# Dummy products in the idle time of TensorE, and a recalibrated queue model, in the prologue of a fused attention and MLP kernel

## The chip, the cores and the metric

One core of a Trainium2 chip. The metric is device time in microseconds (us) of one execution. The kernel before was quoted at 1057.43 us (median of 3 executions, 1055.95 to 1057.48). Every execution also lists its span and the mean granted clock of TensorE (1.0 is full speed).

## The reference, cut to what matters

```python
x = A_x                                   # (1, 2048, 1024) bf16
xn = layernorm(x)                         # no scale, no shift
qkv = xn @ wqkv                           # 32 heads of 32
p = softmax((q @ k^T) * 32**-0.5)         # over 2048 keys, per head
s = (p @ v) @ wo
g = silu(gelu_tanh(layernorm(xn) @ w1 + b1) @ w2 + b2)     # 3584 hidden
return x + s * g
```

The exponentials of the softmax, 32 x 2048 x 2048 of them, run on ScalarE as 1024 instructions of 128 x 1024. They are what the whole kernel is built around.

## The kernel before

The kernel does not write its instructions in order. Every operation is added to a plan; at build time the plan is list-scheduled (step by step, each engine is given the best operation that is ready) with a model of each engine's time, semaphore waits are placed, and each engine then gets its instructions in the order that the model found. **The model decides only the order.** Each engine is handed its list in that order, and in the traces it waits where data is missing (TensorE 0.82 us at 44.79 for a transposing transfer).

The model of a DMA transfer is one queue of a fixed rate and a landing time by kind:

```python
# in _Plan.run(), commit():
if e == "SP":
    ...
    tf[e] = t + o.occ
    state["bw"] = max(state["bw"], t) + o.nbytes / 380.0
    o.fin = state["bw"] + {"w1": WLAT, "w2": WLAT, "tp": 2400.0, "x0": 1900.0, "x1": 1900.0}.get(o.sem[:2], 2300.0)
```

and TensorE takes, at each step of model time `t`, the best candidate that is ready, or sleeps until the next one will be (`nxt`):

```python
# pe_step(t), cut:
for c in cands:
    if c[0] <= t: ...                       # ready: keep the best class
    else:         nxt = min(nxt, c[0])
...
if best is None:
    if nxt < INF:
        wake(nxt, "PE")
    return
```

The prologue turns x into the first keys, queries and values. Sixteen tiles of 128 rows are loaded; VectorE makes their statistics; the normalised tile goes into a ring of four buffers (the profile calls three of them `gw` and one `yT`); tiles 0 and 1 are transposed by TensorE against an identity, tiles 2 to 15 by a transposing DMA into `big`; TensorE then makes K (and Q) of a pair of tiles and V:

```python
for t in (lo, lo + 1):
    if t in DN:        # tiles 2, 3
        xnop[t] = dve(... xnb[t % 4], xst[t] ..., 360, ...)
        continue
    xnop[t] = pool(... xnb[t % 4], xst[t] ..., 950, ...)
for t in (lo, lo + 1):
    ...
    add("SP", lambda e, t=t: e.dma_start_transpose(out=xnT[:, :, t * 128:(t + 1) * 128], in_=xnb[t % 4]),
        1290, 0, [("xnb", t % 4)], [("xnT", t, h) for h in range(2)], 0, sem=f"tp{t % 4}", nbytes=262144)
pro_q.append(k_pair_item(n, False))
...
```

Each engine's list is then issued as it stands:

```python
def emit(self, e, eng, sems):
    for o in self.order[e]:
        for s, v in self.waits[o]:
            eng.wait_ge(sems[s], v)
        ins = o.fn(eng)
        ...
```

The first thing that TensorE does is a warm-up of 13 identity products (`warm_item`). The same DMA queue, that of SyncE, also carries the weights of the MLP. The first six loads of W1 (three pairs of 256 KB each) are held back until a certain tile is normalised, so that they do not crowd the loads of x:

```python
def load_w1(p):
    ...
    for i in range(2):
        ...
        dma(f"w1{gi}{i}", ..., 332000, [], [("w1", gi, i)], 3,
            [xnop[XW + 2 * p]] if p < 3 else [])      # XW = 9: tiles 9, 11, 13
```

After the prologue the first "full unit" of scores starts; from there exponentials, scores, P·V, projections and the MLP run interleaved.

The softmax here doesn't subtract the row's maximum and nothing guards it: scores larger than these inputs give would overflow.

## Time and profile before

| | kernel before |
|---|---|
| span of the profiled execution | 1055.8 us |
| start of the exponentials without a break (first full unit) | 64.6 us |
| from there to the end | 991.2 us |
| TensorE busy from 24.2 to 64.6 us | 38.42 of 40.40 us |
| transposing transfers, issue to landing: least, median, most | 2.9, 4.3, 5.6 us |

The views by stretch, of ScalarE's waits and of TensorE's timeline are in the prediction below. Here is SyncE's part from 36 us on, in the kernel before (start and length of the issuing, line, kind, output and input, how many):

```profile
36.35 1.93 SPq L933 DMA_DIRECT2D w1r<-in_B_w_dram  x2
38.33 0.51 SPq L940 DMA_DIRECT2D w2r<-in_B_w_dram  x1
38.88 3.98 SPq L894 DMA_TRANSPOSE big<-gw  x2
42.90 0.58 SPq L933 DMA_DIRECT2D w1r<-in_B_w_dram  x1
43.52 1.24 SPq L894 DMA_TRANSPOSE big<-gw  x1
44.81 1.34 SPq L894 DMA_TRANSPOSE big<-yT  x1
```

Two blocks of W1 and one of W2, for an MLP whose first product starts at 65.3 us, are issued ahead of the transposes of tiles 12 and 13, and one more W1 ahead of those of 14 and 15. The two transposes at 38.88 took 3.98 us to issue, where the one at 43.52 took 1.24. Their data had been ready: GpSimd's normalisation of tiles 12 and 13 (2.37 us from 35.78 on, on its timeline) ended at 38.15. TensorE's wait at 44.79 (in the prediction's fence) is for these two, tiles 12 and 13, which are pair 6. (The prediction says tile 14 there; that was a slip in counting, for tile 14's transpose is the row at 43.52.)

### The profile page before, as it was taken

Reading aid. Unit: us, or ns where it says so; the run is one execution under the profiler, and the core shown is the slowest. Engines: PE = TensorE matmul, PEld = TensorE weight load, DVE = VectorE, ACT = ScalarE, POOL = GpSimd, SP = SyncE. Lnnn points to the kernel's source line nnn. Section 1 sums busy time; section 2 is a strip of 40 time slices with the busy share of each in tenths; the row PEclk is TensorE's granted clock in tenths of the full one; section 3 lists DMA queues with packets and bytes.
Section 4 is the critical chain, followed back from the end, with each engine's and each line's share of the span. In section 5 each row is a group of like instructions: output and inputs, shape, how many; then the busy total and the mean of one; then the engine's idle time right before and its main releaser. Section 6 shows DMA issues by size and latency. Waiting matters only on the chain.

```text
span 1055.8 us, 31978 instructions
## 1 busy us (share of the span) xinstructions
PE 1024.0 (97%) x14230; PEld 632.8 (60%) x14230; DVE 967.9 (92%) x1463; ACT 1010.3 (96%) x1100; POOL 28.6 (3%) x40
## 2 busy tenths in 40 slices
PE   7998999999999999999999999999999999899997
PEld 4565457656666566656765666556665566564442
DVE  7579899999999989999999999999899999978997
ACT  2779999999999999999999999999999999999994
POOL 3600000000000000000000000000000000000000
PEclk8999999999999999999999999999999999999999
DMA  8955256634275446633565556433664687663322
GB/s 219 232 153 156 56 144 198 184 97 117 86 219 155 135 139 188 166 89 100 160 177 143 146 159 190 135 90 99 179 196 141 192 238 206 193 195 111 124 88 71
DMA packets 302371, 160.16 MB, mean 152 GB/s; under 512 B 40218, under 2 KB 293146, under 8 KB 302234
## 3 DMA queue, kind: packets, MB, share of 16 engines
q1 hardware_dynamic: 302234, 158.12, 53.3%
q8 instruction: 112, 1.84, 0.7%
q14 instruction: 25, 0.20, 0.1%
HBM read 142.35 MB, written 12.06 MB: 146 GB/s over the span
## 4 chain that ended last, share of the span: by engine, by line
ACT 88%; PE 7%; DMA 2%; DVE 2%; SPq 0%; POOL 0%; issue 0%; DVEq 0%; POOLq 0%
ACT P L1134 82%; ACT ut L995 5%; PE ps L701 5%; ACT gw L1031 1%; PE ps L696 1%; PE ps L1120 1%; DMA big<-yT 1%; DMA hT<-in_A_x_dram 1%; DVE ut L854 0%; DMA big<-gw 0%; DVE w1r L1281 0%; DVE V L771 0%; SPq L715 0%; POOL gw L886 0%; SPq L723 0%
## 5 line engine op out<-in xcount | busy, mean ns | idle before, releaser
L1134 ACT ACTIVATE P<-ps 128x1024 bf16<-128x1024 f32 x1024 | 965.3, 1245 | 23.4 <-PE ps L1120 23.3
L1164 DVE TENSOR_TENSOR PA<-P 128x2048 bf16<-128x2048 bf16 x246 | 298.7, 1216 | 15.8 <-ACT P L1134 15.1
L701 PE MATMUL ps<-yT,w1r 128*128 128x256 bf16 x1792 | 231.4, 274 | 3.4 <-DVE nv L1217 1.6
L701 PE MATMUL ps<-w2r,hT 128*128 128x256 bf16 x1792 | 227.2, 274 | 1.6 <-DVE hT L998 0.9
L701 PEld LDWEIGHTS ps<-yT,w1r 128*128 128x128 bf16 x1792 | 162.5, 98 | 58.9 <-issue 30.2
L701 PEld LDWEIGHTS ps<-w2r,hT 128*128 128x128 bf16 x1792 | 162.2, 98 | 53.0 <-issue 31.2
L696 PE MATMUL ps<-P,V 128*32 128x256 bf16 x4096 | 146.5, 274 | 0.0
L1169 DVE TENSOR_TENSOR PA<-PA 128x1024 bf16<-128x1024 bf16 x204 | 138.2, 681 | 1.5
L701 PE MATMUL ps<-big,qk 128*128 128x512 bf16 (+2 forms) x568 | 134.6, 368 | 1.5 <-DMA big<-gw 0.8
L701 PE MATMUL ps<-qk,big 128*128 128x256 bf16 (+1 forms) x736 | 127.3, 306 | 3.2 <-DMA big<-gw 2.7
L696 PEld LDWEIGHTS ps<-P,V 128*32 128x32 bf16 x4096 | 96.5, 96 | 35.6 <-issue 22.6
L1120 PE MATMUL ps<-qk 32*128 32x256 bf16 x2048 | 106.0, 273 | 8.6 <-ACT P L1134 7.6
L1120 PE MATMUL ps<-QKT 32*128 32x256 bf16 x2048 | 101.7, 273 | 2.7 <-ACT P L1134 2.3
L701 PEld LDWEIGHTS ps<-qk,big 128*128 128x128 bf16 x736 | 64.9, 98 | 45.0 <-issue 17.7
L701 PEld LDWEIGHTS ps<-big,qk 128*128 128x128 bf16 x568 | 50.5, 102 | 52.6 <-issue 16.0
L980 DVE TENSOR_TENSOR xb<-ps,b1T 128x512 bf16<-128x512 f32 x112 | 76.4, 685 | 4.7 <-PE ps L701 4.0
L1120 PEld LDWEIGHTS ps<-qk 32*128 32x128 bf16 x2048 | 31.6, 92 | 75.9 <-ACT P L1134 71.6
L1120 PEld LDWEIGHTS ps<-QKT 32*128 32x128 bf16 x2048 | 30.3, 92 | 71.5 <-ACT P L1134 68.5
L995 ACT ACTIVATE ut<-ut 128x1024 f32<-128x1024 f32 x56 | 72.5, 1295 | 0.0
L998 DVE SCALAR_TENSOR_TENSOR hT<-ut,xb 128x1024 bf16<-128x1024 f32 x56 | 67.9, 1212 | 1.3 <-ACT ut L995 1.0
L993 DVE SCALAR_TENSOR_TENSOR ut<-hT,xb 128x1024 f32<-128x1024 bf16 x56 | 68.0, 1214 | 0.0
L696 PE MATMUL ps<-PA,ones 128*32 128x256 bf16 x896 | 46.4, 275 | 0.0
(79 smaller groups left out, 529.7 us busy)
## 6 DMA issues: line engine op xcount, KB each, us to landing
w1r<-in_B_w_dram SPq DMA_DIRECT2D x224, 256.0 KB, 3.5
w2r<-in_B_w_dram SPq DMA_DIRECT2D x128, 448.0 KB, 4.3
qk<-in_A_wqkv_dram SPq DMA_DIRECT2D x16, 256.0 KB, 3.3
g_scratch<-gw SPq DMA_DIRECT2D x32, 128.0 KB, 3.6
o_scratch<-ot SPq DMA_DIRECT2D x56, 64.0 KB, 3.1
big<-o_scratch SPq DMA_DIRECT2D x28, 128.0 KB, 3.7
hT<-in_A_x_dram SPq DMA_DIRECT2D x10, 256.0 KB, 4.2
qk<-in_A_wqkv_dram SPq DMA_DIRECT2D x4, 512.0 KB, 3.7
```

The source lines that it names most:

```text
L696: ins = e.matmul(dst(j), lhsT=lhsT(j), rhs=rhs(j), start=start, stop=stop, tile_position=(0, 32 * j), skip_group_check=True)
L701: return e.matmul(dst, lhsT=lhsT, rhs=rhs, start=start, stop=stop, skip_group_check=True)
L980: dve(lambda e: e.tensor_tensor(xb_t[i2][:, p % 2].rearrange("p (k t) -> p k t", k=2), bank(it.bank).rearrange("p (k t) -> p k t", k=2), b ...
L993: dve(lambda e, r=r: e.scalar_tensor_tensor(ut_t[i2][:, r], h[:, r], 1.0 / GA, xb[:, r], op0=ALU.add, op1=ALU.mult), c_f32(r.stop - r.star ...
L995: act(lambda e: e.activation(ut_t[i2][:], ut_t[i2][:], ACT.Tanh, scale=GC * GA), c_acts(1024), [("ut", i2, 0), ("ut", i2, 1)], [("ut", i2, ...
L998: dve(lambda e, r=r: e.scalar_tensor_tensor(h[:, r], ut_t[i2][:, r], 1.0, xb[:, r], op0=ALU.add, op1=ALU.mult), c_f32(r.stop - r.start), [ ...
L1031: act(lambda e: e.activation(zh, z, ACT.Tanh, scale=0.5), c_acts(1024), [("z", 0), ("z", 1)], [("zh",)], 1)
L1120: ins = e.matmul(bank(b0[j], kk * 256, (kk + 1) * 256), lhsT=QKT[sl][32 * j:32 * j + 32, 1, kb * 128:(kb + 1) * 128], rhs=QKT[sl][32 * j:3 ...
L1134: x = act(lambda e, h=h: e.activation(P[pi][:, 2 * h:2 * h + 2].rearrange("p j k q -> p (j k q)"), ps[:, pr[h] * 1024:(pr[h] + 1) * 1024], ...
L1164: add2.append(dve(lambda e, p0=p0, a0=a0: e.tensor_tensor(PA_all[:, a0:a0 + 2].rearrange("p u j q -> p (u j) q"), P_all[:, p0:p0 + 2, :, 0 ...
L1169: add4.append(dve(lambda e, a0=a0: e.tensor_tensor(PA[a0], PA[a0], PA[a0 + 1], op=ALU.add), c_b16(1024), [("PA", a0 + 1)], [("PA", a0)], P ...
```

## The change

Intent: in the prologue of the kernel before, TensorE runs two stretches at about half clock (0.53 in the prediction's clock column; called cold below), each behind a stretch in which it was mostly idle (busy 1.06 and 1.05 of 3.40 us). So the scheduler puts dummy products (identity times identity, into a free PSUM bank, never read) where its model sees TensorE idle for over 0.3 us, between 6 and 32 us. At the same time the constants of the DMA model are set to longer times. The core of the diff:

```diff
+FILL = 300
+ADJ2 = 0
@@ commit()
-  o.fin = state["bw"] + {"w1": WLAT, "w2": WLAT, "tp": 2400.0, "x0": 1900.0, "x1": 1900.0}.get(o.sem[:2], 2300.0)
+  o.fin = state["bw"] + {"w1": WLAT, "w2": WLAT, "tp": 2800.0, "x0": 2050.0, "x1": 2000.0, "x2": 2500.0}.get(o.sem[:2], 2300.0)
@@ pe_step()
-  cands.append((o.ready, 1, o, None))
+  late = state["mode"] == "f" and state["dopen"] is not None
+  cands.append((max(o.ready, state["cend"]) + ADJ2 if late else o.ready, 1, o, None))
...
   if best is None:
+      if self.fill and t < 32000 and nxt > t + FILL and (t > 6000 or not self.fill[0].left):
+          bf = bank_for(t)
+          if bf is not None and bf[0] <= t:
+              it = self.fill.pop()
+              best = (t, 3, it.chunks[0], (it, bf[1]))
+  if best is None:
       if nxt < INF:
           wake(nxt, "PE")
@@ load_qk(), load_v(): bytes that the model counts
-  dma(f"wqk{i}", ..., 262144 * 8 // 5, ...)
+  dma(f"wqk{i}", ..., 262144 * 2, ...)
-  dma("wv", ..., 665000, ...)
+  dma("wv", ..., 850000, ...)
@@ prologue
+  plan.fill = [fill_item() for _ in range(80)]     # each one 128x512 identity product
@@ normalisation on VectorE, tiles 0, 1 and tiles 2, 3: ns that the model counts
-  75 + 0.26 * 1024
+  455
-  360
+  455
... (bookkeeping of the fills, and marking unused ones as dead: cut)
```

More of the change, by code (lines that the diff above doesn't have):

```diff
@@ L78, in __init__ @@
         self.skip = []
+        self.fill = []
         self.ring_last = {}
@@ L129, in run @@
         state = {"mode": "c", "bw": 0.0, "s": 0, "pv": 0, "pvopen": [], "dopen": None, "susp": None,
-                 "done": 0.0, "last_bank": 7}
+                 "done": 0.0, "cend": 0.0, "last_bank": 7}
         bank_free = {b: [] for b in (4, 5, 6, 7)}
@@ L386, in pe_step @@
                     state["pv"] += 1
+                elif cls == 3:
+                    o.item.k = 1
                 else:
@@ L389, in pe_step @@
                     heads[opening[2]] += 1
-            if cls == 0:
+            if cls == 3:
+                pass
+            elif cls == 0:
                 state["s"] += 1
@@ L401, in pe_step @@
                 it.k += 1
+                if cls == 1:
+                    state["cend"] = start
                 if it.k == len(it.chunks):
@@ L437, in run @@
                 wake(max(t, soon[e][0][0]), e)
+        for it in self.fill:
+            it.chunks[0].dead = True
+            it.chunks[0].start = it.chunks[0].fin = 0.0
         left = [o for o in self.ops if o.start is None]
@@ L722, in load_qk @@
             src = A_wqkv[:, which * D + hg * 128: which * D + (hg + 1) * 128].rearrange("(c p) n -> p c n", p=128)
-            dma(f"wqk{i}", lambda e: e.dma_start(wqk[i], src), 262144 * 8 // 5, [], [("wqk", i)], 3,
+            dma(f"wqk{i}", lambda e: e.dma_start(wqk[i], src), 262144 * 2, [], [("wqk", i)], 3,
                 [xnop[NT - 1]] if nqk["n"] == 3 else [])
@@ L728, in load_v @@
             src = A_wqkv[:, 2 * D + pr * 256: 2 * D + (pr + 1) * 256].rearrange("(c p) n -> p c n", p=128)
-            dma("wv", lambda e: e.dma_start(wv, src), 665000, [], [("wv",)])
+            dma("wv", lambda e: e.dma_start(wv, src), 850000, [], [("wv",)])
         for t in range(XF):
@@ L809, in warm_item, with fill_item @@
             return it
+        def fill_item():
+            it = _Item("fill")
+            chunk(it, lambda e, b: full(e, bank(b), ident[:], ident[:].unsqueeze(1).to_broadcast([128, 4, 128]), True, True), Q512, [("ident",)])
+            return it
         def qk_tile_item(t):
@@ L867, in bass_recurrent_scan__mha_block__mixer_channel_mlp__prompt_kernel @@
                     dve(lambda e, t=t: e.tensor_scalar(xnb[t], xst[t], mv[:, t, 0:1], lnp[:, t, 1:2],
-                                                       op0=ALU.subtract, op1=ALU.mult), 75 + 0.26 * 1024,
+                                                       op0=ALU.subtract, op1=ALU.mult), 455,
                         [XS(t), ("mv", t), ("rs", 0, t)], [("xnb", t)], 0.5)
@@ L882, in bass_recurrent_scan__mha_block__mixer_channel_mlp__prompt_kernel @@
                     xnop[t] = dve(lambda e, t=t: e.tensor_scalar(xnb[t % 4], xst[t], mv[:, t, 0:1], lnp[:, t, 1:2],
-                                                                 op0=ALU.subtract, op1=ALU.mult), 360,
+                                                                 op0=ALU.subtract, op1=ALU.mult), 455,
                                   [XS(t), ("mv", t), ("rs", n)], [("xnb", t % 4)], 0.5)
```

## The prediction

> **What bounds the kernel now.** I read the page first (busy shares and slices), then the busy time of each engine by stretch, then who waited for whom, then the timeline of TensorE in the first 45 us.
>
> Busy time by stretch; the columns are the stretch, its length, the busy time and number of instructions of PE, PEld, DVE, ACT and POOL, the granted TensorE clock, the DMA share and GB/s:
>
> ```profile
> 0.00:24.20 24.20, 17.52 (x119) 10.86 (x120) 17.75 (x52) 5.04 (x6) 7.72 (x17) 0.86 0.84 216
> 24.20:64.60 40.40, 38.42 (x540) 23.11 (x540) 20.02 (x52) 28.29 (x30) 18.62 (x22) 1.00 0.98 210
> 64.60:1041.70 977.10, 961.09 (x13521) 595.66 (x13524) 920.23 (x1345) 977.01 (x1064) 0.00 (x0) 1.00 0.52 149
> 1041.70:1056.00 14.30, 6.98 (x56) 3.20 (x48) 9.87 (x18) 0.00 (x0) 2.28 (x2) 0.83 0.21 74
> ```
>
> The third line carries the argument: from 64.6 to 1041.7 us ScalarE is busy 977.01 of 977.10 us. Its work there is fixed: 992 exponentials left of the 1024, at 15.58 us for 17 (0.916 us each, in the chain of waits), plus the tanh of the MLP and the gate. So the span is a start of 64.6, a body of 977.1 and a tail of 14.1 us. Only start and tail can move, as long as the body stays saturated.
>
> Waits of ScalarE over the whole run (total us, times, longest):
>
> ```profile
> ACT P L1134 <- PE ps L1120: 23.3, 8, 7.0
> ACT big L845 <- PE ps L834: 7.2, 2, 6.4
> ACT L746 <- PEq L1426: 0.7, 1, 0.7
> ```
>
> All of ScalarE's waits are here, and all lie before 64.6: the exponentials wait for score products, that is for TensorE's prologue.
>
> The timeline of TensorE there (start, length, line, output and operands, how many, idle before and releaser):
>
> ```profile
> 1.38 5.64 PE L701 MATMUL ps<-ident 128*128 128x512 bf16 x13 [1.38 <-DVE ident L741]
> 8.00 0.62 PE L834 MATMUL ps<-ident,gw 128*128 128x128 bf16 x8 [0.98 <-DVE gw L867]
> 9.97 0.86 PE L834 MATMUL ps<-ident,gw 128*128 128x128 bf16 x8 [1.35 <-DVE gw L867]
> 10.62 3.38 PE L701 MATMUL ps<-big,qk 128*128 128x128 bf16 x32
> ...
> 19.04 1.05 PE L701 MATMUL ps<-qk,big 128*128 128x256 bf16 x8 [2.73 <-DMA big<-gw]
> 20.33 3.52 PE L701 MATMUL ps<-big,qk 128*128 128x256 bf16 x16 [0.23 <-DMA big<-yT]
> 23.78 0.42 PE L1120 MATMUL ps<-qk 32*128 32x256 bf16 x8
> 24.13 1.05 PE L701 MATMUL ps<-qk,big 128*128 128x256 bf16 x8
> ...
> 31.52 0.39 PE L701 MATMUL ps<-big,qk 128*128 128x256 bf16 x2 [0.40 <-DMA big<-yT]
> ...
> 44.79 0.39 PE L701 MATMUL ps<-big,qk 128*128 128x256 bf16 x2 [0.82 <-DMA big<-gw]
> ```
>
> Compare the two rows of 128x256: sixteen took 3.52 us at 20.33, eight took 1.05 at 24.13. By (length minus one matmul's latency) over (count minus one), that is (3.52-0.42)/15 = 207 ns against (1.05-0.27)/7 = 111 ns each: the first ran at half speed. Cut at steps of about 3.4 us, the clock column (PE alone: stretch, length, busy, clock, DMA) shows the pattern:
>
> ```profile
> 6.60:10.00 3.40, 1.06 (x11) 1.00 1.00 321
> 10.00:13.40 3.40, 3.40 (x35) 0.53 0.99 332
> 13.40:16.85 3.45, 2.91 (x33) 0.97 0.25 89
> 16.85:20.25 3.40, 1.05 (x8) 1.00 1.01 198
> 20.25:23.70 3.45, 3.37 (x16) 0.53 1.07 169
> ```
>
> A stretch with one microsecond of products is followed by one at about half clock; one with three is followed by full clock. The two cold stretches hold exactly the products on which the first long run of exponentials waits.
>
> [...] Here a transposing transfer lands 2.9 us after issue at best and 4.3 us at the median, and the kernel's model adds 2.4 us to its queue time: low, as the diff assumes.
>
> **The change part by part.**
> Removed: nothing that computes. The program is ordered at build time by a model of all engines, so the edits to the model change the order of instructions and not their work.
>
> 1. Fills. Up to 80 identity products of 512 columns may be put where the model sees TensorE idle for over 0.3 us, a bank free, between 6 and 32 us of model time (the chip starts about 0.7 us later). The gaps over 0.3 us in that range are 0.98 + 1.35 + 2.73 + 0.40 = 5.46 us; at 0.216 us each some 23 fills, and I expect 15 to 30. They lie in idle time and by themselves cost nothing, except an overrun of at most one fill where the model's gap is too long: three or four gaps, half a fill on average, 0.3 to 0.5 us.
> 2. What the fills buy, first cold stretch. The 32 products of 128 columns run at (3.38-0.31)/31 = 99 ns each; the warm pace for 128 columns is about half of 111, 56 ns: 31 x 43 ns = 1.35 us, and (0.86-0.31)/7 = 78 against 56 for 7 of the second eight transposes 0.15. Sum 1.5 us. It gets to the next stage through VectorE: the casts out of PSUM at 12.58 and 14.12 stand in its queue ahead of the normalisation of tiles 2 and 3 (15.13 to 16.12), whose transposing transfers TensorE awaits at 19.04. VectorE idled 0.47 and 0.97 us before these casts, so 1.4 of the 1.5 can pass.
> 3. Second cold stretch. Sixteen at 207 become sixteen at 111: 15 x 96 = 1.4 us, plus 0.15 of the latency (0.42 to 0.27): 1.6 us, directly on the path to the score products at 23.78 and to the long run of exponentials at 24.23.
> 4. Recalibration: tile transfers +100 to +200 ns, transposing ones +400, weight loads 1.10 to 1.38 us and 1.75 to 2.24 us of queue (bytes over 380 per ns), normalisation 341 or 360 to 455 ns (the trace shows 0.53 to 0.54 with its latency). It should stop TensorE from being parked in front of transfers that the model thought landed: 0.40 + 0.82 us at 31.52 and 44.79. I count 0.4 of these 1.2.
> 5. The rule with ADJ2 does nothing: it is a maximum with the start of an earlier product, always in the past, plus zero.
>
> From 24.2 to 64.6 TensorE is busy 38.42 of 40.40 us, so an earlier arrival there should carry through to the first full unit at 64.6. VectorE had 0.86 + 0.47 + 0.80 us of waits for TensorE between 21 and 34 us and so can follow most of it. Sum at 64.6: -1.4 -1.6 -0.4 +0.4 = -3.0 us, perhaps -0.2 more in the tail since a tuned change was presumably kept for its best order: 1057.43 - 3.2 = 1054.2 us.
>
> **The rivals.**
> (a) The saved time turns into a wait for transfers. At 44.79 TensorE waits for the transpose of tile 14, behind a chain of statistics on VectorE, normalisation on GpSimd and the transfer. For it: VectorE is 4.95 of 5 us busy from 25 to 30 us. Against it: that chain passes VectorE's casts of TensorE's results, which come earlier too, and 19.28 us of TensorE work follow 44.7. If it wins, about 1 us is left: 1056.4.
> (b) Fills delay real products. In-order TensorE runs every fill; if the model believes in later transfers than there are (3.5 us issue to landing in the new model, 3.2 to 3.4 in the trace for the first two), fills run past the landing. At 5 extra fills, 1.1 us is lost: 1055.3.
> (c) The new order disturbs the body or tail. Every tie in 977 us is decided anew, and TensorE is 98% busy there. A late score product starves ScalarE, and the 14.1 us tail hangs on 24 output products and VectorE. For: tuned constants stay as they were. Against: zero waits of ScalarE in the body, so there is slack. Plus or minus 1 to 2 us: 1052 to 1057.
> (d) Only the clock phase matters: [...]some executions may already have one cold stretch less. The three times spread by 1.5 us. The gain would then vary by that.
>
> **Range and chances.** Ideal carry-through without overrun and with both parked waits gone gives -1.5 -1.6 -1.2 = -4.3, with a lucky tail -6: 1051.4. (a) with (b), or a bad tail, give 1056.8. Predicted 1054.2 us, 8 in 10 between 1051.4 and 1056.8. Two per cent are 21 us, two thirds of all the time ScalarE waits at all; hardly reachable, and nothing in the change can cost as much unless the body breaks. Faster 0.01, same 0.985, slower 0.005.
>
> **What would show it right or wrong.** After: rows of identity products of 512 columns between 7 and 20 us, 216 ns apart; the clock at 1.00 in all stretches from 7 to 25 us; the 16 products of pair 1 in about 1.95 us; the start of the saturated stretch at 61 to 62 us; ScalarE still without waits until the tail, which stays near 14 us. It is wrong if the clock is full and the saturated stretch still begins at 63.5 or later (rival a or b: look for idle time before DMA-released products, or fills adjacent to ready work), if new ScalarE waits appear after it, or if the tail differs by more than 1 us.

The sum: it came to -3.0 us at 64.6, and with 0.2 us for the tail to 1054.2 us. Of what it reckons with, the traces show the following. The 0.216 us of a product of 512 columns: in the kernel before, five at 60.24 take 1.24 us and one 0.38, (1.24-0.38)/4 = 215 ns. The 56 ns of a product of 128 columns was an estimate, half of the measured 111; the changed kernel then took (1.96-0.22)/31 = 56 ns. The clock: in the kernel before it goes to half at 10.2, back at 13.6, to half at 20.4 and back at 23.9 us. That every fill is run: the changed kernel has 36 identity products of 512 columns, 13 of the warm-up and 23 fills.

## The result, and the profile after

In the first comparison the changed kernel took 1059.43 us (median of 4; 1057.37 to 1060.73) and the kernel before 1057.45 (median of 4; 1055.95 to 1057.48). The ratio is 1.002, with a 95% interval of 1.0002 to 1.0039. All ratios and intervals here are from the fast runs of the same rounds; they are not quite the ratio of the medians that are quoted, nor of the means. The class "within 2%" was right; the gain of 3 us was not there, and 1059.4 lies above the range. A repetition in other rounds gave 1.0002 (experiment e1), so the fair statement is: no gain, and nothing lost that is sure.

The busy time by stretch of the changed kernel, with the columns of the prediction's first fence:

```profile
0.00:24.20 24.20, 21.24 (x159) 11.62 (x159) 19.32 (x56) 7.08 (x9) 8.60 (x18) 1.00 0.93 235
24.20:64.60 40.40, 36.71 (x526) 22.02 (x522) 19.21 (x48) 26.63 (x29) 17.74 (x21) 1.00 0.92 199
64.60:1041.70 977.10, 961.56 (x13540) 596.12 (x13544) 920.23 (x1344) 976.55 (x1064) 0.00 (x0) 1.00 0.52 149
1041.70:1056.00 14.30, 6.50 (x44) 2.73 (x32) 9.40 (x18) 0.00 (x0) 2.28 (x2) 0.84 0.21 75
```

In the first stretch the clock went from 0.86 to 1.00, and 159 products ran where 119 had. In the second, TensorE is busy for 36.71 us instead of 38.42: it came in earlier and then **waited more** (it is idle for 3.69 us of the stretch instead of 1.98). Body and tail are as before (976.55 and 977.01 us of ScalarE; the half microsecond is the earlier start).

TensorE's timeline in the changed kernel, same columns as before (line numbers are 20 to 26 higher):

```profile
1.38 6.84 PE L721 MATMUL ps<-ident 128*128 128x512 bf16 x18 [1.38 <-DVE ident L761]
...
9.78 1.96 PE L721 MATMUL ps<-big,qk 128*128 128x128 bf16 x32
...
14.29 2.55 PE L721 MATMUL ps<-ident 128*128 128x512 bf16 x11
17.11 1.05 PE L721 MATMUL ps<-qk,big 128*128 128x256 bf16 x8 [0.27 <-DMA big<-gw]
19.33 1.92 PE L721 MATMUL ps<-big,qk 128*128 128x256 bf16 x16 [1.18 <-DMA big<-yT]
...
33.82 0.83 PE L721 MATMUL ps<-big,qk 128*128 128x256 bf16 x6 [0.94 <-DMA big<-gw]
...
43.59 0.61 PE L721 MATMUL ps<-big,qk 128*128 128x256 bf16 x4 [1.10 <-DMA big<-gw]
```

The eleven fills at 14.29 run (2.55-0.38)/10 = 217 ns apart, with 0.38 for the latency of one: full clock. The 32 products of 128 columns take 1.96 us (3.38 before), the sixteen of pair 1 take 1.92 (3.52 before). So both cold stretches are gone, by the amounts predicted. But look at the brackets: 1.18 us of waiting for a transposing DMA at 19.33, 0.94 at 33.82, 1.10 at 43.59.

Where the exponentials begin, first long run and first full unit, on ScalarE's timeline; the kernel before:

```profile
24.23 7.44 ACT L1134 ACTIVATE P<-ps 128x1024 bf16<-128x1024 f32 x8 [7.05 <-PE ps L1120]
64.61 12.94 ACT L1134 ACTIVATE P<-ps 128x1024 bf16<-128x1024 f32 x14 [6.43 <-PE ps L1120]
```

and the changed kernel:

```profile
22.06 5.61 ACT L1160 ACTIVATE P<-ps 128x1024 bf16<-128x1024 f32 x6 [7.05 <-PE ps L1146]
64.14 12.94 ACT L1160 ACTIVATE P<-ps 128x1024 bf16<-128x1024 f32 x14 [6.76 <-PE ps L1146]
```

This is the whole result in four rows. The first long run came **2.17 us earlier**, and the first full unit, from which ScalarE never rests, only **0.47 us earlier**. The rest of the 2.17 was lost on the way:

| step of TensorE | before | after | gained so far |
|---|---|---|---|
| first long run of exponentials | 24.23 | 22.06 | 2.17 |
| pair 6 (tiles 12, 13) released by its transposes | 44.79 | 43.59 | 1.20 |
| first full unit (ScalarE's row) | 64.61 | 64.14 | 0.47 |

From the release at 44.79 to the score products of the first full unit (64.17) the kernel before needs 19.38 us; the changed kernel from 43.59 to 63.69, 20.10. The recalibrated order has left 0.7 us more of TensorE's work behind that wait.

The changed kernel has 23 fills (5 of them join the warm-up). Apart from the fills, 106 of the 6054 places of TensorE's list hold another operation than before, 39 of VectorE's, 6 of SyncE's and 2 of GpSimd's, all in the prologue; ScalarE's list is the same. The order of body and tail is identical.

### The profile page after: what moved, and what is told of

It is laid out like the page before. It is cut to its first block, busy times and chain, and to the rows that moved or that the text cites. A ratio compares the mean times of both kernels' runs of the same rounds, so it can differ in the third digit from the quotient of the medians.

```text
span 1055.3 us, 32024 instructions
## 1 busy us (share of the span) xinstructions
PE 1026.0 (97%) x14253; PEld 632.5 (60%) x14253; DVE 968.2 (92%) x1463; ACT 1010.3 (96%) x1100; POOL 28.6 (3%) x40
## 4 chain that ended last, share of the span: by engine, by line
ACT 88%; PE 6%; DVE 3%; DMA 1%; POOL 1%; issue 0%; DVEq 0%; SPq 0%
ACT P L1160 82%; ACT ut L1021 5%; PE ps L721 4%; DVE ut L880 1%; ACT gw L1057 1%; PE ps L716 1%; PE ps L1146 1%; DMA big<-yT 1%; DVE w1r L1307 0%; POOL lnp L934 0%; DMA hT<-in_A_x_dram 0%; DVE lnp L898 0%; DVE V L791 0%; POOL gw L912 0%; DVE mv L882 0%
## 5 line engine op out<-in xcount | busy, mean ns | idle before, releaser
L721 PE MATMUL ps<-big,qk 128*128 128x512 bf16 (+2 forms) x568 | 131.7, 360 | 3.3 <-DMA big<-gw 2.0
L721 PEld LDWEIGHTS ps<-big,qk 128*128 128x128 bf16 x568 | 48.1, 98 | 54.4 <-issue 16.0
```

The lines of the kernel that those rows point to most:

```text
L721: return e.matmul(dst, lhsT=lhsT, rhs=rhs, start=start, stop=stop, skip_group_check=True)
```

## The experiments

The first theory after the result: **T1**, transfers bound the prologue from 24 to 64 us, so that a TensorE which comes earlier waits longer for the transposing transfers (rival (a) of the prediction). Rivals: **T2**, the new order of the prologue costs what the fills gain; **T3**, the clock: new idle time after 32 us, where no fill is allowed, makes new cold stretches. Here is what all twelve runs gave; "first full unit" is from each run's one trace, the clocks are the means of single executions. The kernel before in the same rounds had medians of 1058.14 (e1 to e4), 1058.40 (e5 to e8) and 1058.27 (e9, e10).

| run | what it is | median us | lowest to highest | ratio to before, 95% | clocks | first full unit |
|---|---|---|---|---|---|---|
| e1 | changed kernel again | 1058.09 | 1056.57–1061.80 | 1.0002 [0.9984, 1.0020] | .993–.999 | 65.57 |
| e2 | fills alone | 1056.92 | 1055.80–1059.62 | 0.9989 [0.9976, 1.0002] | .998–.999 | 64.86 |
| e3 | recalibration alone | 1059.23 | 1054.87–1060.88 | 1.0003 [0.9986, 1.0019] | .992–.997 | 66.55 |
| e4 | changed, W1 gated later | 1062.32 | 1057.22–1065.15 | 1.0029 [1.0004, 1.0054] | .989–.998 | 70.06 |
| e5 | changed, 5 dummies in two more gaps | 1057.99 | 1057.24–1059.18 | 0.9990 [0.9974, 1.0005] | .998–.999 | 65.30 |
| e6 | fills alone, MLP loads moved back | 1054.65 | 1054.32–1055.35 | 0.9957 [0.9941, 0.9973] | .998–.999 | 61.24 |
| e7 | before, MLP loads moved back | 1055.21 | 1054.68–1056.44 | 0.9965 [0.9948, 0.9982] | .995–.996 | 61.44 |
| e8 | changed, loads moved, 5 dummies | 1055.73 | 1054.92–1057.16 | 0.9969 [0.9953, 0.9984] | .997–.999 | 61.99 |
| e9 | fills alone, four of six loads moved | 1054.98 | 1054.32–1056.73 | 0.9975 [0.9961, 0.9988] | .997–.999 | 61.60 |
| e10 | changed, loads moved | 1056.05 | 1055.09–1060.52 | 0.9997 [0.9975, 1.0018] | .995–.999 | 61.78 |
| e11 | before again, one look | 1059.19 | – | – | .995 | 65.94 |
| e12 | before a third time, one look | 1058.06 | – | – | .994 | 64.81 |

The mean clock counts cold stretches. One stretch of 3.4 us at half speed takes 3.4 x 0.5 / 1056 = 0.0016 off it (an estimate from the clock column). The tail takes a share too: from 1041.7 us on its clock was 0.77 (e6) to 0.93 (e2; 0.83 in the kernel before), which is up to 0.003. The traced executions with no step of half clock in the prologue show .998 or .999 (the changed kernel, e2, e5, e6; e8, at .997, has one in the body), with one .996 (e7), with two .994 or .995 (the kernel before, e1, e11, e12), with three .994 (e3), with five .990 (e4). So, roughly, .998 is a run without a cold stretch ahead of the tail, .995 has two of them, .993 three (the last an estimate from the 0.0016 of one); where they lie, only a trace tells.

In all traces but e3, e5 and e8 the time from the first full unit to the end is 991.1 to 991.3 us (991.6, 991.8 and 993.0 in these three, where ScalarE has one or two waits of 0.3 to 1.1 us in the body, though its order is unaltered). So a version is judged by its prologue. The 1.8 us that e8's trace loses in the body lie behind a cold stretch there, which is told with e8.

### e1: the changed kernel again

No edit.

> The changed kernel unaltered, for its spread and a second trace. Four executions so far ran 1057.4 to 1060.7 us, the kernel before 1056.0 to 1057.5. Theory T (transfers): the time saved on the clock turns into waits for the transposing transfers of the last tiles, so the first full unit starts at 63 to 66 us and the median lies 0 to 3 us above before, with a spread of 2 us or more that sits in the start, not in the body. Rival C (the body or tail is disturbed): a slower execution would show the start at 64.1 again and ScalarE waits after it.

Measured: 1058.09 us, ratio 1.0002. The loss of 0.2% of the first comparison did not return, and neither did a gain appear. The executions split by clock: three at .998 or .999 took 1056.6 to 1057.2 us, three at .993 to .995 took 1058.9 to 1061.8. The profiled one was of the second kind. TensorE's timeline in it, at the wait for pair 4 (tiles 8 and 9), then PE's stretches (the stretch, its length, PE's busy time and count, granted clock, DMA share, GB/s):

```profile
33.74 0.83 PE L721 MATMUL ps<-big,qk 128*128 128x256 bf16 x6 [1.86 <-DMA big<-gw]
```

```profile
32.00:34.00 2.00, 0.26 (x3) 1.00 0.88 211
35.00:42.00 7.00, 7.00 (x73) 0.52 1.07 245
```

The same products waited 0.94 us in the first trace and 1.86 here, and after the longer wait TensorE ran at 0.52 of its clock for 7 us, with 73 products where the first trace had 112. The kernel that was to end the cold stretches made a new one, because its earlier TensorE meets the transfers at 33 us with empty hands. This speaks for T3 **as a consequence of T1**: the cold came behind the wait.

### e2 and e3: each half alone

```diff
 e2:  (constants of the model as before the change; plan.fill = [80 fills] kept)
 e3:  -plan.fill = [fill_item() for _ in range(80)]
      +plan.fill = []
```

> The fills alone: the numbers of the model as before, so the order of all real instructions is that of before with 19 identity products added. Theory T: the first long run of exponentials starts about 2 us earlier, as in the changed kernel, and the first full unit still at 63.5 to 65; time within 1 us of before. Rival R (the recalibrated order costs the time and the fills earn it): the first full unit at 61.5 to 62.5 and 2 to 3 us faster than before (1054.5).

> The recalibration alone, no fills: cold stretches are back. Rival R: 2 to 4 us slower than before (1059.5 to 1061.5). Theory T: within 1.5 us of before, as the first cold stretches are hidden behind transfers anyway. If fills themselves cost (rival F), this one is faster than the changed kernel by 1 us or more.

Measured: e2 0.9989 and e3 1.0003, each with an interval that holds 1. The program of e2 is the order of the kernel before plus 19 fills and nothing else, so it isolates the clock. All its six executions ran at .998 or more; its first long run of exponentials came at 22.85, 1.38 us before that of the kernel before. Then:

```profile
45.04 0.39 PE L721 MATMUL ps<-big,qk 128*128 128x256 bf16 x2 [3.00 <-DMA big<-gw]
```

TensorE waits **3.00 us** where the kernel before waited 0.82, and is released at 45.04 where the other was released at 44.79. The first full unit comes at 64.86, against 64.61. Of the time that the fills saved ahead of this point nothing passed it in this trace. That is T1 without help from a new order. Some 1 us of mean gain (0.9989) stays possible within the interval; the trace does not show it.

e3 has no fills: clocks .992 to .997, a wait of 2.11 us ahead of the release at 43.39, a new cold stretch behind it, and the first full unit at 66.55. Its release is 1.4 us earlier than that of the kernel before (43.39 against 44.79), which goes with the new order of the transfers, and it gains nothing by it either. T2 as the only cause falls: e2 has the old order and no gain in its trace. The order's 0.7 us behind the wait, told above, remains as a second term.

### e4: gating the W1 loads later

```diff
-                    [xnop[XW + 2 * p]] if p < 3 else [])
+                    [xnop[NT - 1]] if p < 3 else [])
```

> The changed kernel with the first six loads of W1 (256 KB each) held back until the last tile is normalised, so five of them no longer stand in the transfer queue ahead of the last transposing transfers. Theory T: the last transpose lands 2 to 4 us earlier than 48.4, the first full unit starts 1.5 to 3 us earlier and the time falls by 1.5 to 3 us against the changed kernel. If TensorE's own work is the bound after 44 us, nothing moves (within 0.7 us).

Measured: 1062.32 us, ratio 1.0029, the slowest of all: a miss as a gain. The transposes of tiles 12, 14 and 15 were issued at 34.54, 38.78 and 40.13 us instead of 36.98, 42.25 and 43.53, so the edit did to the queue what it should (two loads of W2 still stood ahead of them). But TensorE's stretches read:

```profile
32.00:34.00 2.00, 0.27 (x6) 1.00 0.82 180
35.20:52.70 17.50, 17.50 (x147) 0.51 0.97 241
```

A wait of 1.73 us ahead of 33.87 was followed by 17.5 us at half clock, through which TensorE is listed as busy without a break. Four of the six executions have such a clock (.989 to .991, 1061.4 to 1065.2 us). The two at .998 took 1057.2 us, no better than the changed kernel at the same clock. The run is inconclusive about the queue, because the clock broke first and because a new gate also gives the scheduler a new order; it is why e6 moves the loads in the finished program instead.

### e5: dummies in the two remaining gaps

```diff
 # emit(), ahead of the waits of an operation
+n = self.gaps.get(o, 0) if e == "PE" else 0
+if n:
+    (wait for VectorE's readers of the bank)
+    for _ in range(n):
+        self.dummy(eng, o.item.bank)      # identity product of 512 columns
...
+plan.gaps = {tiles[i]: n for i, n in {6: 5, 8: 5}.items()}     # ahead of pairs 4 and 6
```

> The changed kernel with five more identity products (5 x 0.216 = 1.1 us) put directly ahead of each of the two groups before which TensorE was seen waiting 0.9 to 1.9 us for a transposing transfer (pairs 4 and 6, near 33 and 43 us). Theory G (the gap tips the clock): no stretch at half clock between 7 and 60 us in the trace, mean clock 0.998 or more in every execution, the first full unit at 63.5 to 64.5, spans 1054.5 to 1055.5, median 1057 and a spread under 1.5 us, against 1056.6 to 1061.8 for the changed kernel. Rival (the slow executions come from transfers): the spread of 4 us or more stays at a mean clock of 0.998.

Measured: 1057.99 us, ratio 0.9990, clocks all .998 or .999, spread 1.9 us where the changed kernel had 5.2 in e1. So the dummies do end the new cold stretches, as T3 says. But in the trace the wait of pair 6 still ends at 45.04, after 1.51 us of idle time behind five dummies, and the first full unit is at 65.30, where 63.5 to 64.5 was expected: a miss. With the clock at full speed in every execution the kernel is still no faster than before. The clock alone is not what holds 64 us in place.

### e6 and e7: the MLP loads behind the last transpose

The loads of W1 and W2 that the program issues ahead of the last transposing transfer are moved directly behind it, in the finished order; TensorE's order stays as it is. (The expectations speak of five loads, 1.5 MB. It was six: five blocks of W1 of 256 KB and one of W2 of 448 KB, 1.7 MB.)

```diff
 plan.run(HG * 64, SLACK)
+held = [o for o in sp[:tp[-1]] if o.sem[:2] in ("w1", "w2")]   # sp: SyncE's order, tp: its transposes
+(take `held` out of the order, put it in behind sp[tp[-1]])
 plan.settle()
```

> Fills alone, in the order of before, with the five loads of the MLP's weights (four of W1, one of W2, 1.5 MB) that stood in the transfer queue ahead of the last transposing transfers put directly behind them; TensorE's order is unchanged. Theory T: the wait of 3.00 us before pair 6 shrinks to under 1 us, the first full unit starts 2 to 3 us earlier than 64.9, and the time is 2 to 3 us below before (1055 to 1056). If the transfers are paced by something else (the ring of four normalised tiles, GpSimd), the wait stays over 2 us and the time within 1 us of fills alone (1056.9).

> The kernel before with the same five loads moved, no fills. Theory T: TensorE waits only 0.82 us there, so at most 0.8 us can be had: time 0 to 1 us below before. If the queue itself is worth more than the clock, it gains as much as with fills (2 us or more).

Measured: e6, with the fills and the old constants, 1054.65 us (0.9957), **the fastest of all, and faster than both kernels**; six executions within 1.0 us. SyncE's queue in e6, TensorE's first products of pair 6, and ScalarE's first full unit:

```profile
34.52 4.85 SPq L920 DMA_TRANSPOSE big<-gw  x3
39.41 2.29 SPq L920 DMA_TRANSPOSE big<-yT  x1
41.75 2.23 SPq L959 DMA_DIRECT2D w1r<-in_B_w_dram  x4
```

```profile
41.42 0.39 PE L721 MATMUL ps<-big,qk 128*128 128x256 bf16 x2
```

```profile
61.24 12.94 ACT L1160 ACTIVATE P<-ps 128x1024 bf16<-128x1024 f32 x14 [6.42 <-PE ps L1146]
```

The last transpose (tile 15) begins its issue at 39.41, not at 44.81 (before) or 44.94 (e2). Some 1.2 us of this were there already at tile 8's transpose (26.91 against 28.12 in e2), ahead of every moved load: that part is the difference of two executions. The row of TensorE has no bracket: no wait at all, at 41.42 instead of 45.04 in e2. TensorE is busy for 11.50 of the 11.50 us from 33.5 to 45 (8.54 in e2, the same order). TensorE came to pair 6 only 0.62 us earlier than in e2 (41.42 against 45.04 - 3.00 = 42.04); the other 3.00 us of the 3.62 by which the first full unit came earlier are the wait that is gone. The first full unit is at 61.24, within the "61 to 62 us" of the prediction, but by another road: the prediction had it from the fills with the loads in place.

e7 has no fills, and got 1055.21 us (0.9965). I had expected at most 0.8 us from it, since TensorE without fills would be the later one; the mean gain over the kernel before of these rounds (1058.95) is 3.4 us: a miss, and an instructive one. Even the kernel before waits for this queue: 0.82 us in its first trace, 1.29 and 2.28 in its two others (e12 and e11). With the loads moved, no wait of TensorE for a transfer is left after the one of 0.40 us at 29.23 in e7's prologue. Its traced execution had one cold stretch and its first long run of exponentials at 21.63, so part of its early first full unit (61.44) is luck of the clock; the mean of 3.4 us over five executions is not one execution's luck. Nor is it all waiting: the six executions of the kernel before in these rounds with e7's clock or a little more (.995 to .997) have a mean of 1057.4, which leaves 1.9 us; the other five ran at .993 or .994 and took 1060.2 to 1061.3, which none of e7's did.

What the fills add once the queue is cleared is e6 against e7, of the same rounds, with means of 1054.71 and 1055.56: **0.8 us**, and a spread of 1.0 instead of 1.8. The standard error of this difference, from the two spreads, is about 0.4 us, and the intervals of the two ratios overlap: likely, not sure.

### e8, e9, e10: the same with the new constants, and with fewer loads moved

```diff
 e8:   changed kernel + loads moved + gaps {6: 5}
 e9:   e6 with  held = [o for o in sp[tp[-5]:tp[-1]] if ...]     # four loads, 1.2 MB
 e10:  changed kernel + loads moved
```

> The changed kernel with the five loads moved and five identity products ahead of pair 4 only. Theories T and G together: last transposes land 3 us earlier, the wait of 1.1 us before pair 6 is gone, no half clock, first full unit at 62 to 63, time 1055 to 1056.5 with a spread under 1.5 us. If TensorE's work after 44 us is all that counts, 1057.

> A smaller dose: fills alone, with only the last four of the six MLP loads (three of W1, one of W2, 1.2 MB; the loads moved before were six, five of W1 and one of W2, not five as was written) put behind the last transposing transfer, and the first two W1 loads left ahead of tile 10. Theory T, with the wait at pair 6 the one that sets the start: most of the gain of the full move stays, first full unit within 1.5 us of 61.2 and time 1055 to 1056; the clock stays warm as no wait over 1.5 us is left. If only the whole move helps (the first two loads delay tiles 10 and 11, which hold the ring of four tiles), the time is over 1056.2.

> The changed kernel in its recalibrated order with all six loads moved and no further identity products. Theory T: 2 to 3 us below the changed kernel (1055 to 1056.5), as with the five products ahead of pair 4 (1055.7); if the clock still tips at the wait before pair 4, some executions show a mean clock of 0.995 or less and 1058 us or more. The order of before with fills and the same move ran 1054.65: if the recalibrated order costs by itself, this one stays 0.5 us or more above.

Measured: e9 1054.98 us (0.9975), its first full unit at 61.60; the longest wait of TensorE in its trace from 6 us on is 1.21 us, and that execution's clock .998. The four loads that lie between the last five transposes are enough, as far as the intervals of two sets of rounds can tell. e10 0.9997: four of six executions at .998 or more took 1055.1 to 1056.7 us, and two at .995 took 1060.4 and 1060.5, which spoils the mean. e8, the same with five dummies ahead of pair 4, had none of these (all .997 or more) and got 0.9969, with a spread of 2.2 us where under 1.5 was expected. e10 and e8 ran in different rounds, so what the dummies are worth in time is not measured; that no execution with them fell to .995 is. Nor does .997 always tell of the prologue. In e8's traced execution (.997) the prologue is at full clock, and the one cold stretch ahead of the tail lies in the body: a clock of 0.55 from 907.80 to 911.20 us, and ScalarE waits 1.10 us for scores at 914.27. With the loads moved the recalibrated constants are no better than the old ones (e9 against e10 in the same rounds: 0.9975 against 0.9997).

### e11 and e12: the kernel before again

No edit; one look each, state unknown.

> The kernel before unaltered, for a second trace: 14 of its 33 timed executions so far ran at a mean clock of 0.994 or less and 1057.9 to 1061.3 us. Theory G: a slower execution shows a third half-clock stretch after 24 us, behind a wait for a transposing transfer; a fast one (1057 to 1058) shows the two early ones only and a start at 64 to 65 us.

> The same kernel before a third time, since one execution may fall on either side. Same expectation: the mean clock tells how many half-clock stretches the trace shows, and the span less the start of the first full unit is 991.2 us either way (rival: a slow execution loses its time in the body).

Measured: e12 repeats the first trace: first long run at 24.26, release of pair 6 at 44.99 after 1.29 us, first full unit at 64.81. e11 is the better find. Its clock changed at other moments (to half at 18.4 us, where the kernel before in its first trace went to half at 10.2 and 20.4), so that it had one early cold stretch instead of two, and its first long run came at 22.44, as early as if it had fills. TensorE's timeline at pair 6, then its stretches, in e11:

```profile
44.65 0.39 PE L701 MATMUL ps<-big,qk 128*128 128x256 bf16 x2 [2.28 <-DMA big<-gw]
```

```profile
42.00:44.70 2.70, 0.42 (x10) 1.00 0.99 192
45.90:49.10 3.20, 3.20 (x52) 0.50 1.22 170
```

The kernel before, with the same gain by luck, loses it in the same place: released at 44.65 instead of 44.79, and then punished by a cold stretch of 3.2 us, so that its first full unit (65.94) is *later* than that of the execution that started 1.8 us behind it. No fill and no new constant is needed for the effect.

Put the releases of pair 6 beside each other, for kernels whose queue is as it was: 44.79 (idle 0.82), 44.99 (1.29), 44.65 (2.28), 45.04 (3.00, e2); with the new order 43.59 (1.10), 43.39 (2.11, e3), 45.04 (1.51 behind five dummies, e5). TensorE's idle time there ranges over more than 2 us, the release over 0.4 us among the first four. TensorE arrives when it likes; the queue decides when it leaves.

## Why the prediction was wrong, step by step

**Right.** The number of fills (23, "some 23"; partly luck, for the prediction's own 5.46 us at 0.216 each make 25, and the gap of 0.40 us at 31.52 got none), their pace (217 ns, where five products of 512 columns in the kernel before ran 215 ns apart), the two cold stretches and their sizes: 3.38 to 1.96 us is 1.42 (predicted 1.35), 3.52 to 1.92 is 1.60 (predicted 1.6). The clock of 1.00 throughout from 7 to 24 us. The body fixed, the tail at 14 us. That the rule with ADJ2 does nothing: programs built with and without it are the same, instruction for instruction.

**The step that failed.** "From 24.2 to 64.6 TensorE is busy 38.42 of 40.40 us, so an earlier arrival there should carry through to the first full unit at 64.6." It carried 0.47 of 2.17 us, and in e2, with nothing but fills, none. The clock was full and the saturated stretch began after 63.5, which is the sign of being wrong that the prediction itself had named. A busy share of 95% is also what TensorE shows when it is *just* late enough not to wait. The wait of 0.82 us at 44.79 is where two chains met, and it showed that the other chain (statistics, normalisation, transposing transfer through a queue with 1.7 MB of weights in it) was already the later one. Moving TensorE alone earlier lengthens such a wait: 0.82 became 3.00 in e2. The counterproof is e6: the same order of TensorE, the queue cleared, and the release at 41.42 with no wait.

**Rival (a) happened in full**, and the prediction named the right place for it (but for the tile: 12 and 13, not 14). It dismissed it for two reasons. One, that the chain ahead of the transfer would come earlier too, since VectorE's casts would: in e2, whose order is the old one, it did not (45.04 against 44.79). The other, that 19.28 us of TensorE's work follow: true, but work behind a wait does not shorten it. It looked at VectorE and GpSimd in that chain and not at the SyncE queue, whose six rows held the answer.

**A smaller failure on the way to 24 us**: steps 2 and 3 were added as if independent, 3.0 us, and gave 2.17. The normalisation of tiles 2 and 3 ended 2.6 us earlier (13.48 instead of 16.12), more than expected, but the transfers landed only 0.99 us earlier (19.29 instead of 20.28): the issue of tile 2's transpose took 2.70 us instead of 1.35. That is the queue again. Some 0.4 us (my estimate from their row of 0.60 us for four, less the latency) went to four V products that stand ahead of the first scores.

**Step 4, the recalibration**, was credited with 0.4 us. It should have kept TensorE from parking in front of transfers. The changed kernel parks for 0.94 and 1.10 us where the one before parked for 0.40 and 0.82, since its model, even with the new constants, expects tile 13's transpose landed at 39.9 us and tile 15's at 42.1 in the trace's time (read from the plan, plus the 0.7 us by which the chip starts later), and the trace has the pairs behind them released at 43.59 and 48.4. A model of one rate and fixed landings misses the queue by about 4 and 6 us; 400 ns more do not mend that. For the same reason the fills cannot fill these gaps: allowing them up to 70 us of model time adds two near 60 us and none at 33 or 43 us, for the model sees no gap there.

**Rival (d), the clock phase**, was right in that executions of one kernel differ in their cold stretches (the kernel before has two early ones in its first trace and one in e11), and it is larger than thought, for there are cold stretches after 32 us too (0.52 from 35 to 42 us in e1), where the prediction did not look: the executions of the changed kernel at .998 or more lie at 1056.6 to 1057.4, those at .997 or less at 1058.9 to 1061.8 (ten executions). The kernel before shows the same over 33 timed executions: 19 at .995 or more have a mean of 1057.6, 14 at .994 or less one of 1059.8. The traces also show what goes with the clock. All clock changes of one trace lie on one grid of steps of 3.41 us (the kernel before: 10.2, 13.6, 20.4 and 23.9 us, and 1051.3 in the tail). Placed on it, TensorE's stretch ahead of the cold one of e1, and then the two across which the gap of 3.00 us in e2 lies, after which the clock stayed full, read:

```profile
31.93:35.34 3.41, 1.60 (x14) 1.00 1.00 236
40.10:43.51 3.41, 1.94 (x23) 1.00 1.12 248
43.51:46.92 3.41, 1.88 (x50) 1.00 1.12 240
```

So it is the work inside a grid step that went with the clock, and a long gap that is shared by two steps did no harm. **Rival (c)** was wrong in its ground ("every tie in 977 us is decided anew": no place of body or tail changed). **Rival (b)** left no trace that I could tell from the rest.

**Open.** What sets the 2 us of spread that remain at full clock (e5), and whether it comes with the transfers: one trace cannot tell. The executions of the first comparison at .997 with 1059.0 to 1060.7 us were not traced; one cold stretch explains .997 but no trace shows where it lay, and e8's trace shows that it can lie in the body. Whether the fills alone are worth their 1 us: 0.9989 with 1 just inside the interval.

## What to carry to other kernels

A dummy product bought clock here, and no time by itself: before giving an engine back some microseconds, find the next place where it waits for someone else, and read that someone's queue to the end, because the short wait of a busy engine (0.82 us, at 38.42 busy of 40.40) marked the point here where another chain was already the later one. Loads that nobody needs for another 20 us have no business ahead of transfers that the next stage awaits, even when a model finds room for them; moving six of them behind the last transpose was worth about 3.4 us with no other edit, and the fills then added some 0.8, just at the edge of the noise. Where half clock follows idle time, as here (0.52 for 7 us behind a wait of 1.86 us in e1), look at the clock of each single execution, for a median mixes executions with and without a cold stretch.

## What the traces show of the clock and the queue

- Waits of TensorE that were followed by half clock: 1.73 us (e4), 1.86 (e1), 2.11 (e3), 2.28 (e11). One of 3.00 us (e2) was not, and those of 0.94, 1.10, 1.29 and 1.51 us (after, e12, e5) were not either. TensorE's work within a step of the grid went with the clock: on each trace's grid of 3.41 us, the clock fell to half after steps with 0.59 (e7) to 1.72 us (e4) of work in the prologue, while 1.88 and 1.94 (e2) and 1.90 (e5) kept the full clock. In between it is not clean: 1.50 kept it in e11 (4.80 to 8.21) and 1.72 in e7 (6.71 to 10.12), and 2.03 lost it once, in the body of e8, behind gaps of no more than 0.88 us. The length of the gap alone does not tell.
- How long the half clock lasts differs, too. The two cold stretches of the kernel before lasted 3.4 us each (10.2 to 13.6, 20.4 to 23.9). In e1 TensorE ran at 0.52 of its clock for 7 us and in e4 at 0.51 for 17.5 us while it was listed as 100% busy, with score and P·V products of 32 rows or columns among the full ones. Why is not shown by a run here.
- The issue of one transposing transfer behind other traffic took 1.24 us for tile 14 in the kernel before and 3.58 for tile 11 in e2, and the landing came 2.9 to 5.6 us after the start of the issue (median 4.3, before); with 1.7 MB of loads taken out of its way in the same queue the last transpose was issued 5.5 us earlier (39.41 in e6 against 44.94 in e2, same order of TensorE; 1.2 us of it were there ahead of the moved loads).
- The build-time model of the queue, one rate of 380 bytes per ns and a fixed landing time, missed two transposes by about 4 and 6 us, while the fills (217 ns) and the two cold stretches (1.42 and 1.60 us gained, 1.35 and 1.6 predicted) went as computed.
